# A new written-out order for a transformer block: another order table, a table of buffer slots, 75 operations on other engines, and another split of w_mod's rows over the partitions

## The chip, the cores and the metric

The kernel runs on one core of a Trainium2 chip. The metric is the device time of one execution in microseconds (us). A core has five instruction queues: TensorE (PE, with its weight loads, PEld), ScalarE (ACT), VectorE (DVE), GpSimd (POOL) and SyncE (SP), which here only issues DMA transfers; ACT issues a few DMAs too. Each queue runs in the order in which it was written, and an instruction whose inputs are not there holds up everything behind it on its queue.

## The reference, cut to what matters

The inputs are bf16: x is 2048 rows by 640, attention has 32 heads of 20 with a causal window of 256 rows, the MLP has 1536 hidden columns.

```python
mod = (silu(c) @ w_mod).reshape(1, 6, 1, 640)      # w_mod: 640 x 3840, c: 1 x 640
sa, ca, ga, sb, cb, gb = mod[:, 0], ..., mod[:, 5]
h = layernorm(x) * (1 + ca) + sa
q, k, v = split_heads(h @ wqkv)                    # 640 -> 3 x 32 x 20
p = softmax(where(0 <= i - j < 256, q @ k.T * 20 ** -0.5, -1e9))
x = x + ga * (merge_heads(p @ v) @ wo)
h = layernorm(x) * (1 + cb) + sb
x = x + gb * ((sigmoid(h @ w_gate) * (h @ w_up)) @ w_down)
```

## The kernel before, in words

The 2048 rows are worked in eight chunks of 256 rows, a = 0 to 7. Each chunk goes through the same stages, and the stages of neighbouring chunks are interleaved so that TensorE always has something to do:

- **Head of the program.** c and the first pieces of w_mod are loaded. A small matmul (L634) puts c onto the partitions as five columns, silu(c) is formed (L636 to L640), and its product with w_mod gives the six modulation rows. Row k of w_mod meets element k of c, so both have to lie on the same partition. The rows of the two gates, ga and gb, go through DRAM and come back broadcast to all partitions: `gate<-gq`, then `gbc<-gate`. ga is multiplied into wo (`wos`, L1253), gb into the twelve 128-row pieces of w_down (`wds`, L1192, 128 x 640 each); w_down is needed only by the last matmul of a chunk.
- **LN and modulation.** Statistics on DVE (L776, L778), the power on POOL (L781 to L788), the normalised rows (L793, L796), a transposing DMA on SP's queue (`hT<-x`, L803) and the scale and shift of each transposed piece (`amodu` for attention, `bmodu` for the MLP: L811 on ACT, L812 on DVE).
- **QKV.** `projq`, `projk` and `projv` multiply `hT` by wqkv. The results leave PSUM by copies (`evqk`, `evv`: L893 on ACT, L894 on DVE) into `stg`, `QT`, `KT` or `V`; from `stg`, queries and keys are transposed by DMA on SP's queue.
- **Scores.** For each half of the heads (q = 0, 1) a chunk forms four sets of scores, a block of 24 or 32 small matmuls each (`S<-QT,KT`, L669). There is one PSUM buffer `S` for scores: a set can be written only when the exponentials (L1015, ACT) of the set before it have read it. POOL masks the exponentials (L1040). P times V is one burst of 64 matmuls (`M<-E,V`), joined in one instruction group with the first score set of the next half.
- **Normalising and the way to wo.** DVE transposes, divides and transposes back (L1082, L1087, L1089, L1091). The heads are then regrouped through DRAM: four DMAs a half write `doc<-On` (`n_ow`), two DMAs a chunk read `oT<-doc` on SP's queue, the first (128-row tiles 0 and 1) after the first half, the second (tiles 2 to 4) after both. For chunk 0 the eight writes are issued from ACT's queue. Then comes `wo` (`M<-wo,oT`, five matmuls for 128 rows and 320 columns) and the residual (L1164).
- **MLP.** `mlpg` and `mlpu` (`M<-h2T,wg`, `M<-h2T,wu`) fill two of four PSUM banks M; ACT takes the tanh that stands for the sigmoid (L1209), DVE the product (`glu`, L1211, `hh<-sig,M`), which frees them; `down` (`M<-wd,hh`) and the second residual (L1230) end the chunk.

Projections, matmuls of wo and the MLP stand between the score sets to cover the exponentials.

What sets the order: the program is recorded as 2121 operations (907 for PE, 333 for ACT, 424 for DVE, 264 for POOL, 193 for SP). The table `PRIO` holds one number for each; sorted, they give one order of the whole program, and the remainder by 5 names the engine. `schedule()` goes through the operations in that order and appends each to its engine's queue. It also keeps estimated times (durations, the constants `SWITCH`, `OVERLAP`, `QMAX`, `MIXED`, `START`), which serve one purpose only: where a tile has several buffers it takes the one that these estimates free first. `emit()` then writes the queues and puts semaphore waits on what is not ordered already.

Of the kernel before, what the change touches and what calls it, by code (L numbers as in the profile page):

```python
# [17 lines left out]
NDT = D // 128  # L18
# [7 lines left out]
SWITCH = 0.095  # L26
ENGATTR = {"pe": "tensor", "act": "scalar", "dve": "vector", "pool": "gpsimd", "sp": "sync"}
ENGS = ("pe", "act", "dve", "pool", "sp")
OVERLAP = {"pe": 0.0, "act": 0.085, "dve": 0.075, "pool": 0.045, "sp": 0.0}
# [52 lines left out]
class Prog:  # L82
# [69 lines left out]
    def schedule(self):  # L152


        free = {e: START for e in ENGS}
        bw = 0.0
        lastturn = False
        order = {e: [] for e in ENGS}
        dmacnt = [0] * NDMA
        dmalast = [None] * NDMA  # L160
        rr = 0
        pemode = 0
        portend = 0.0
        freed = {}

        def slot_time(pool, s):
            ten = pool.tenant[s]
            if ten is None:
                if not all(x.done for x in pool.init[s]):
                    return None  # L170
                return max([x.end + x.lat for x in pool.init[s]], default=0.0)
            return None if ten.left else freed[ten]

        def take(t, s):
            ten = t.pool.tenant[s]
            t.prev = list(t.pool.init[s]) if ten is None else list(ten.rel)
            t.slot = s
            t.pool.tenant[s] = t

        for o in sorted(self.ops, key=lambda x: x.prio):  # L180
            assert all(d.done for d in o.deps), o.tag
            e = ENGS[o.prio % 5]
            assert e in o.engs, (o.tag, e)
            o.eng = e
            st = max([o.tmin, free[e] + (SWITCH if e == "pe" and o.mode != pemode else 0.0)]
                     + [d.end + (0.0 if d.eng == "pe" and e == "pe" else d.lat) for d in o.deps])
            if o.isdma and e == "sp":
                st = max(st, bw - QMAX)
            for t in o.tiles:
                if t.slot is None:  # L190
                    step = 1 if t.mate is None else 2
                    best = None
                    for s in range(0, len(t.pool.tenant), step):
                        rts = [slot_time(t.pool, s + k) for k in range(step)]
                        if None not in rts and (best is None or max(rts) < best[0]):
                            best = (max(rts), s)
                    assert best is not None, (o.tag, t.name)
                    if t.mate is None:
                        take(t, best[1])
                    else:  # L200
                        take(t, best[1] + t.odd)
                        take(t.mate, best[1] + 1 - t.odd)
                for x in t.prev:
                    st = max(st, x.end + x.lat)
            if e == "dve" and o.port:
                st = max(st, free["pool"])
            elif e == "pool":
                st = max(st, portend)
            o.start = st
            if e == "pe":  # L210
                pemode = o.mout
            dur = o.dur[e]
            free[e] = st + dur - OVERLAP[e]
            if e == "dve" and o.port:
                portend = free[e]
            if o.isdma:
                turn = o.dlat > 3.0
                if e == "sp" and bw - st > 2.0:
                    free[e] += 0.35 if o.dur[e] > 1.0 else 0.1
                bw = max(st + o.dlat, bw + (MIXED if turn != lastturn and bw > st + o.dlat else 0.0)) + o.work  # L220
                lastturn = turn
                o.end = max(bw - 0.83, st + dur)
                s = rr
                rr = (rr + 1) % NDMA
                dmacnt[s] += 16
                o.key, o.val = f"d{s}", dmacnt[s]
                if dmalast[s] is not None:
                    o.deps.append(dmalast[s])
                dmalast[s] = o
            else:  # L230
                o.end = st + dur
            order[e].append(o)
            o.done = True
            for t in o.tiles:
                t.left -= 1
                if t.left == 0:
                    last = {}
                    for x in t.ops:
                        if x.isdma:
                            last[x] = x  # L240
                    for e2 in ENGS:
                        xs = [x for x in t.ops if x.eng == e2 and not x.isdma]
                        if xs:
                            last[e2] = max(xs, key=lambda x: x.start)
                    t.rel = list(last.values())
                    freed[t] = max(x.end + x.lat for x in t.rel)
        self.order = order
        self.span = max(o.end for o in self.ops)
# [88 lines left out]
def c_pe(n):  # L337
# [3 lines left out]
PE_EPS = 0.14  # L341
PRIO = [
# [124 lines left out]
START = 0.8  # L467
PORTLAG = 0.05
MIXED = 0.55
# [837 lines left out]
```

## Time and profile before

| what | value |
|---|---|
| median of 3 runs | 325.76 us (325.64 to 326.33) |
| span of the profiled execution | 324.3 us, granted clock 1.000 |
| what lies around the span | 325.76 - 324.3 = about 1.5 us |
| PE busy | 317.3 us, 98% |
| ACT, DVE, POOL busy | 212.3 (65%), 211.8 (65%), 187.2 us (58%) |
| DMA | 71694 packets, 37.85 MB |

The span counts from the first to the last instruction of the profiled execution; the measured time also holds what lies around it. Busy shares are averages over stages that differ: the first 90 us load weights and fill the pipeline, the middle is steady, and the last is a tail without new attention work. In a row of the timeline the first number is the start in us, the second the length, and the bracket gives the idle time just before it with the instruction that ended it. Lines are those of the kernel before.

### The profile page before, as it was taken

How to read it: one execution, taken by the hardware profiler on the slowest of the kernel's cores; microseconds unless marked ns; L12 is line 12 of the kernel's file. 1: busy time of each engine (PE TensorE's matmuls, PEld its weight loads, DVE VectorE, ACT ScalarE, POOL GpSimd, SP SyncE). 2: the span in 40 equal slices, each digit the busy share in tenths (PEclk: the TensorE clock that was granted, in tenths of full speed). 3: DMA queues.
4: the chain of work that ended last, by engine and by line, in shares of the span. 5: the costliest groups of instructions: out<-in, count | busy, mean ns of one | idle time of the engine just before them, and what ended most of it. 6: DMA issues, size and time to landing. Idle time of an engine off the chain costs nothing.

```text
span 324.3 us, 11594 instructions
## 1 busy us (share of the span) xinstructions
PE 317.3 (98%) x4872; PEld 222.7 (69%) x4873; DVE 211.8 (65%) x424; ACT 212.3 (65%) x316; POOL 187.2 (58%) x276
## 2 busy tenths in 40 slices
PE   8999999989999999999999999999999999999997
PEld 3564545446776568765776467877786788787885
DVE  5797898778687959674477475837463769264332
ACT  1899985889876687788687867786767764011120
POOL 5128869976668694847585939382939691012100
DMA  7998799989891383824405394340213032202101
GB/s 249 371 333 299 165 269 180 200 137 183 260 164 22 83 109 77 152 61 101 85 22 82 97 103 110 92 69 5 81 40 88 3 79 53 76 20 64 40 2 40
DMA packets 71694, 37.85 MB, mean 117 GB/s; under 512 B 45274, under 2 KB 70362, under 8 KB 71642
## 3 DMA queue, kind: packets, MB, share of 16 engines
q1 hardware_dynamic: 69616, 35.31, 48.3%
q10 hardware_dynamic: 2026, 1.80, 2.1%
q8 instruction: 38, 0.62, 0.8%
q14 instruction: 14, 0.11, 0.1%
HBM read 21.30 MB, written 5.25 MB: 82 GB/s over the span
## 4 chain that ended last, share of the span: by engine, by line
PE 73%; DMA 2%; SPq 2%; DVE 1%; POOL 1%; issue 0%; DVEq 0%
PE M L668 61%; PE S L669 6%; PE M L669 5%; DMA gbc<-gate 2%; SPq L803 2%; DVE wd L1192 1%; POOL x L793 0%; POOL st L788 0%; DVE hh L1211 0%; POOL E L1040 0%; DVE x L1230 0%; DVEq L310 0%
## 5 line engine op out<-in xcount | busy, mean ns | idle before, releaser
L1040 POOL TENSOR_SCALAR_AFFINE_SELECT E<-E 128x512 bf16<-128x512 bf16 (+1 forms) x176 | 142.6, 836 | 68.7 <-ACT E L1015 67.0
L1015 ACT ACTIVATE E<-S 128x512 bf16<-128x512 f32 (+2 forms) x184 | 150.9, 878 | 47.4 <-PE S L669 46.5
L668 PE MATMUL M<-wqkv,hT 128*128 128x480 bf16 (+1 forms) x340 | 73.9, 355 | 0.6 <-ACT hT L846 0.5
L668 PE MATMUL M<-h2T,wu 128*128 128x256 bf16 x480 | 68.0, 273 | 0.5 <-DVE hh L1211 0.5
L668 PE MATMUL M<-h2T,wg 128*128 128x256 bf16 x480 | 67.8, 273 | 0.0
L668 PE MATMUL M<-wd,hh 128*128 128x320 bf16 (+2 forms) x396 | 58.1, 295 | 0.0
L1209 ACT ACTIVATE sig<-M 128x512 f32<-128x512 f32 x48 | 28.9, 602 | 44.1 <-PE M L668 41.7
L1211 DVE SCALAR_TENSOR_TENSOR hh<-sig,M 128x512 bf16<-128x512 f32 x48 | 32.4, 681 | 37.1 <-ACT sig L1209 24.0
L668 PEld LDWEIGHTS M<-h2T,wu 128*128 128x128 bf16 x480 | 45.9, 98 | 8.4 <-issue 1.2
L668 PEld LDWEIGHTS M<-h2T,wg 128*128 128x128 bf16 x480 | 45.7, 98 | 7.1
L668 PEld LDWEIGHTS M<-wqkv,hT 128*128 128x128 bf16 x340 | 30.1, 98 | 27.6 <-DMA wqkv<-in_A_wqkv_dram 1.6
L668 PEld LDWEIGHTS M<-wd,hh 128*128 128x128 bf16 x396 | 36.8, 98 | 14.3 <-DVE hh L1211 0.2
L669 PEld LDWEIGHTS S<-QT,KT 20*64 20x64 bf16 (+1 forms) x1856 | 19.9, 100 | 21.3 <-ACT E L1015 12.0
L1230 DVE TENSOR_TENSOR x<-M,x 128x320 bf16<-128x320 f32 (+2 forms) x33 | 15.6, 476 | 27.2 <-PE M L668 27.2
L669 PE MATMUL S<-QT,KT 20*64 20x256 bf16 (+5 forms) x1856 | 32.1, 228 | 1.2 <-ACT E L1015 1.2
L776 DVE BATCH_NORM_STATS2 st<-x 128x6 f32<-128x320 bf16 x64 | 28.6, 477 | 2.3 <-DMA x<-in_A_x_dram 1.9
L1082 DVE STREAM_TRANSPOSE T<-M 128x512 f32<-128x512 f32 x32 | 21.5, 698 | 9.2 <-PE S L669 8.0
L668 PE MATMUL M<-wo,oT 128*128 128x320 bf16 x160 | 25.4, 299 | 0.0
L669 PE MATMUL M<-E,V 128*32 128x128 bf16 (+1 forms) x960 | 22.8, 246 | 0.8 <-ACT E L1015 0.4
L781 POOL TENSOR_SCALAR st<-st 128x2 f32<-128x2 f32 x16 | 3.7, 234 | 33.8 <-DVE st L778 33.6
L669 PEld LDWEIGHTS M<-E,V 128*32 128x32 bf16 x960 | 19.2, 97 | 5.3 <-issue 2.9
L1091 DVE STREAM_TRANSPOSE On<-Tn 128x1024 bf16<-128x1024 bf16 x16 | 19.8, 1240 | 0.3
(77 smaller groups left out, 240.2 us busy)
## 6 DMA issues: line engine op xcount, KB each, us to landing
x<-in_A_x_dram SPq DMA_DIRECT2D x23, 160.0 KB, 2.3
doc<-On SPq DMA_DIRECT2D x56, 40.0 KB
wd<-in_B_w_down_dram SPq DMA_DIRECT2D x4, 480.0 KB
wd<-in_w_mod_dram SPq DMA_DIRECT2D x5, 320.0 KB
wqkv<-in_A_wqkv_dram SPq DMA_DIRECT2D x4, 400.0 KB
wu<-in_w_mod_dram SPq DMA_DIRECT2D x5, 320.0 KB
oT<-doc SPq DMA_DIRECT2D x8, 192.0 KB, 2.5
out_dram<-x SPq DMA_DIRECT2D x9, 160.0 KB
```

Source lines behind the costliest of these rows:

```text
L668: return e.matmul(o, l, r, start=st, stop=sp, skip_group_check=True)
L669: return e.matmul(o, l, r, start=st, stop=sp, tile_position=tp, skip_group_check=True)
L776: A("dve", lambda e, g, bi=bi, j=j: e.bn_stats(v(bi * 12 + j * 6, 6), src[bi].ap[:, j * 320:(j + 1) * 320]), 0.48, reads=[src[bi].r()], wr ...
L781: A("pool", lambda e, g: e.tensor_scalar(v(28, n), var(), EPS, None, op0=ALU.add), 0.2, reads=[st.r(("m", bi)) for bi in range(n)], writes ...
L803: return e.dma_start_transpose(dst(), src())
L1015: A("act", lambda e, eng: e.activation(dst(), src(), ACT.Exp, scale=SM_SCALE), c_act(n), reads=[Sp.r()], writes=[E.r(key)], prio=3, tag=f" ...
L1040: A("pool", lambda e, eng: e.affine_select(rows(dst), rows(src), pattern=[[0, 8], [sign, n]], compare_op=ALU.is_ge, fill=0.0, base=base, c ...
L1082: A("dve", lambda e, g, h=h: e.transpose(T1.ap[:, 512 * h:512 * h + 512], X[h].ap), 0.694, reads=[X[h].r()], writes=[T1.r(h)], prio=3.5, t ...
L1091: A("dve", lambda e, g: e.transpose(On.ap[:], Tn.ap[:]), 1.22, reads=[Tn.r()], writes=[On.r()], prio=4, tag=f"tr2_{a}")
L1209: A("act", lambda e, g, pg=pg, sg=sg: e.activation(sg.ap[:], pg.ap[:], ACT.Tanh, scale=0.5), c_act(512), reads=[pg.r()], writes=[sg.r()], ...
L1211: A("dve", lambda e, g, pu=pu, sg=sg, f0=f0: e.scalar_tensor_tensor(out=hh.ap[:, f0:f0 + 2, :], in0=sg.ap[:].rearrange("p (a b) -> p a b", ...
L1230: A("dve", lambda e, g, ps=ps, bi=bi, c0=c0, n=n: e.tensor_tensor(x1[bi].ap[:, c0:c0 + n], ps.ap[:, 0:n], x1[bi].ap[:, c0:c0 + n], op=ALU. ...
```

## The change

Three things change.

**Order and engines.** `PRIO` is another table. 75 operations are on another engine, all of them among `evqk`, `evv`, `evqt`, `amodu`, `bmodu`, `ahTe` and one `wds`. PE keeps 907 operations and SP 193; ACT goes from 333 to 331, DVE from 424 to 433, POOL from 264 to 257. SP's queue is word for word the same. On every engine the first 21 us of the program keep their order.

**Slots.** A second table `SLOTS` names the buffer of each tile; the estimates in `schedule()` and their constants are gone.

**c and w_mod.** c is read as 128 pieces of five elements in place of five pieces of 128; w_mod's row 5p+t lies on partition p in column block t, where before row 128t+p lay there. Sizes and numbers of w_mod's pieces stay, their distance in DRAM becomes 5 rows of 7680 bytes instead of one.

```diff
 def schedule(self):
-    free = {e: START for e in ENGS}
...
     for o in sorted(self.ops, key=lambda x: x.prio):
         e = ENGS[o.prio % 5]
-        st = max([o.tmin, free[e] + (SWITCH if e == "pe" and o.mode != pemode else 0.0)]
-                 + [d.end + (0.0 if d.eng == "pe" and e == "pe" else d.lat) for d in o.deps])
...
         for t in o.tiles:
             if t.slot is None:
-                step = 1 if t.mate is None else 2
-                best = None
...
+                s = SLOTS[tiles[t]] if SLOTS else 0
+                ten = t.pool.tenant[s]
+                t.prev = list(t.pool.init[s]) if ten is None else list(ten.rel)
+                t.slot = s
+                t.pool.tenant[s] = t
...
 PRIO = [
-    23, 28, 258, 8, 43, 33, 718, 18, 1218, 38, 3, 507, 513, 72, 67, 48, 53, 58, 76, 84, 101, 99, 144, 149, 154, 159,
+    23, 28, 258, 8, 43, 33, 958, 18, 1448, 38, 3, 507, 513, 72, 67, 48, 53, 58, 76, 84, 101, 99, 144, 149, 154, 159,
...
+SLOTS = [
...
-    c_row = p_oT.aps[0][0:NDT, 0, 0:128]
+    c_pt = p_oT.aps[0][:, 0, 0:NDT]
...
-    dma(lambda: c_row, lambda: c.rearrange("o (t p) -> (o t) p", p=128), 0.05, writes=[R_crow], prio=-1, eng="act", lat=0.3)
-    wm_src = w_mod.rearrange("(t p) f -> p t f", p=128)
+    dma(lambda: c_pt, lambda: c.rearrange("o (p t) -> (o p) t", t=NDT), 0.05, writes=[R_cpt], prio=-1, eng="act", lat=0.3)
+    wm_src = w_mod.rearrange("(p t) f -> p t f", t=NDT)
...
-    e.matmul(psc.ap[:, 0:NDT], c_row, ident[0:NDT, 0:NDT], start=True, stop=True)
+    e.matmul(psc.ap[:, 0:NDT], ident[:], c_pt, start=True, stop=True)
```

Three places of the new order follow. The first is TensorE, the second half of chunk 1's scores (from about 42.6 us in the profile of before): an edge set of 32 score matmuls, two sets of 24, and the projections (`M<-wqkv,hT`) between them. Before:

```order
L669 MATMUL S<-QT,KT 128x64 x32
L668 MATMUL M<-wqkv,hT 128x480 x15
L669 MATMUL S<-QT,KT 64x256 x8
L669 MATMUL S<-QT,KT 64x192 x8
L669 MATMUL S<-QT,KT 64x64 x8
L668 MATMUL M<-wqkv,hT 128x480 x9
L669 MATMUL S<-QT,KT 64x256 x8
L669 MATMUL S<-QT,KT 64x192 x8
L669 MATMUL S<-QT,KT 64x64 x8
L668 MATMUL M<-wqkv,hT 128x480 x15
```

And now:

```order
L635 MATMUL S<-QT,KT 128x64 x32
L634 MATMUL M<-wqkv,hT 128x480 x12
L635 MATMUL S<-QT,KT 64x256 x8
L635 MATMUL S<-QT,KT 64x192 x8
L635 MATMUL S<-QT,KT 64x64 x8
L634 MATMUL M<-wqkv,hT 128x480 x12
L635 MATMUL S<-QT,KT 64x256 x8
L635 MATMUL S<-QT,KT 64x192 x8
L635 MATMUL S<-QT,KT 64x64 x8
L634 MATMUL M<-wqkv,hT 128x480 x13
```

The projections between the sets are 12, 12 and 13 matmuls in place of 15, 9 and 15.

The second place is ScalarE at the same time, about 45 to 53 us: the exponentials (`E<-S`), copies out of PSUM, and the four writes `doc<-On` of chunk 0's second half. Before:

```order
L893 ACTIVATE stg<-M 128x16x20
L893 ACTIVATE V<-M 128x8x20
L1015 ACTIVATE E<-S 128x4x2x192
L1015 ACTIVATE E<-S 128x8x64
L570 DMA doc<-On 20x4x256 x4
L1015 ACTIVATE E<-S 128x8x64
L1015 ACTIVATE E<-S 128x4x2x192
L893 ACTIVATE stg<-M 128x24x20
```

And now:

```order
L981 ACTIVATE E<-S 128x8x64
L981 ACTIVATE E<-S 128x4x2x192
L859 ACTIVATE V<-M 128x24x20
L981 ACTIVATE E<-S 128x8x64
L981 ACTIVATE E<-S 128x4x2x192
L536 DMA doc<-On 20x4x256 x2
L859 ACTIVATE V<-M 128x24x20
L536 DMA doc<-On 20x4x256
L981 ACTIVATE E<-S 128x8x64
L536 DMA doc<-On 20x4x256
L981 ACTIVATE E<-S 128x4x2x192
```

Before, all four writes stand behind the exponentials of the first set of 24 after the edge set. Now two stand behind those of the second, one behind a copy, and the last behind the first half of the exponentials of the third set.

The third place is VectorE from about 80 us: the products of chunk 0's MLP (`hh<-sig,M`), the scaling of w_down (`wd<-wd,gbc`), and the transposes (`T<-M`) that begin the normalising of chunk 2's first half. Before:

```order
L1211 SCALAR_TENSOR_TENSOR hh<-sig,M 128x512
L1192 TENSOR_TENSOR wd<-wd,gbc 128x640 x4
L1211 SCALAR_TENSOR_TENSOR hh<-sig,M 128x512 x3
L1192 TENSOR_TENSOR wd<-wd,gbc 128x640 x4
L1082 STREAM_TRANSPOSE T<-M 128x512 x2
L1211 SCALAR_TENSOR_TENSOR hh<-sig,M 128x512
```

And now:

```order
L1177 SCALAR_TENSOR_TENSOR hh<-sig,M 128x512
L860 CAST stg<-M 128x16x20
L860 CAST V<-M 128x8x20
L1158 TENSOR_TENSOR wd<-wd,gbc 128x640
L1177 SCALAR_TENSOR_TENSOR hh<-sig,M 128x512
L1158 TENSOR_TENSOR wd<-wd,gbc 128x640
L742 BN_STATS st<-x 128x6
L1177 SCALAR_TENSOR_TENSOR hh<-sig,M 128x512
L1158 TENSOR_TENSOR wd<-wd,gbc 128x640 x2
L1177 SCALAR_TENSOR_TENSOR hh<-sig,M 128x512
L1158 TENSOR_TENSOR wd<-wd,gbc 128x640
L742 BN_STATS st<-x 128x6
```

One scaling of w_down stands ahead of the second product where four stood; behind these rows come four more scalings and then the two transposes, so that nine stand ahead of the transposes in place of eight, with two statistics among them.

More of the change, by code (lines that the diff above doesn't have):

```diff
@@ L25 @@
 NDMA = 24
-SWITCH = 0.095
 ENGATTR = {"pe": "tensor", "act": "scalar", "dve": "vector", "pool": "gpsimd", "sp": "sync"}
 ENGS = ("pe", "act", "dve", "pool", "sp")
-OVERLAP = {"pe": 0.0, "act": 0.085, "dve": 0.075, "pool": 0.045, "sp": 0.0}
 class Res:
@@ L152, in schedule @@
     def schedule(self):
-        free = {e: START for e in ENGS}
-        bw = 0.0
-        lastturn = False
         order = {e: [] for e in ENGS}
@@ L161, in schedule, with number @@
         rr = 0
[L162 to L178, printed above, removed]
+        tiles = {}
+        def number(t):
+            if t is not None and t not in tiles:
+                tiles[t] = len(tiles)
+                number(t.mate)
+        for o in self.ops:
+            for t in o.tiles:
+                number(t)
         for o in sorted(self.ops, key=lambda x: x.prio):
@@ L184, in schedule @@
             o.eng = e
-            st = max([o.tmin, free[e] + (SWITCH if e == "pe" and o.mode != pemode else 0.0)]
-                     + [d.end + (0.0 if d.eng == "pe" and e == "pe" else d.lat) for d in o.deps])
-            if o.isdma and e == "sp":
-                st = max(st, bw - QMAX)
             for t in o.tiles:
                 if t.slot is None:
-                    step = 1 if t.mate is None else 2
-                    best = None
[L193 to L215, printed above, removed]
-            if o.isdma:
[L217 to L223, printed above, removed]
-                rr = (rr + 1) % NDMA
[L225 to L231, printed above, removed]
+                    s = SLOTS[tiles[t]] if SLOTS else 0
@@ new lines, in schedule @@
+                    ten = t.pool.tenant[s]
+                    assert ten is not None or all(x.done for x in t.pool.init[s]), (o.tag, t.name)
+                    assert ten is None or ten.left == 0, (o.tag, t.name)
+                    t.prev = list(t.pool.init[s]) if ten is None else list(ten.rel)
+                    t.slot = s
+                    t.pool.tenant[s] = t
+            if o.isdma:
+                dmacnt[rr] += 16
+                o.key, o.val = f"d{rr}", dmacnt[rr]
+                if dmalast[rr] is not None:
+                    o.deps.append(dmalast[rr])
+                dmalast[rr] = o
+                rr = (rr + 1) % NDMA
@@ L237, in schedule @@
                     last = {}
[L238 to L244, printed above, removed]
+                    for x in sorted(t.ops, key=lambda x: x.prio):
+                        last[x if x.isdma else x.eng] = x
                     t.rel = list(last.values())
-                    freed[t] = max(x.end + x.lat for x in t.rel)
         self.order = order
-        self.span = max(o.end for o in self.ops)
     def emit(self):
@@ L338, in c_pe @@
     return max(n, 64) / 2400.0 + 0.0027
-PE_EPS = 0.14
 PRIO = [
[3 rows of a table removed]
[3 rows of a table added]
     92, 87, 187, 237, 242, 247, 253, 263, 272, 267, 280, 275, 290, 300, 305, 286, 317, 296, 322, 311, 376, 357, 386,
[1 row of a table removed]
[1 row of a table added]
     541, 495, 501, 665, 677, 480, 485, 491, 565, 570, 576, 545, 551, 630, 652, 525, 555, 561, 625, 660, 681, 685,
[111 rows of a table removed]
[111 rows of a table added]
+]
+SLOTS = [
[20 rows of a table added]
 ]
@@ L466 @@
 DSAFE = 1.5
-START = 0.8
-PORTLAG = 0.05
-MIXED = 0.55
 NPB = 0
@@ L484 @@
 WSE = (("dve", "pool"), ("dve", "pool"))
-QMAX = 4.5
 WDT = 72.0
@@ L558, in build @@
     R_w3 = [R(f"wqkv{i}") for i in range(12)]
-    R_crow, R_ident, R_ccol, R_cth, R_siluc, R_silubc, R_wo = (R(n) for n in ("crow", "ident", "ccol", "cth", "siluc", "silubc", "wo"))
+    R_cpt, R_ident, R_ccol, R_cth, R_siluc, R_silubc, R_wo = (R(n) for n in ("cpt", "ident", "ccol", "cth", "siluc", "silubc", "wo"))
     R_wg = [[R(f"wg{t}_{h}") for t in range(NDT)] for h in range(2)]
@@ L633, in build @@
     psc = Tile(p_M, "psc")
-    p_oT.init[0].append(A("pe", lambda e, g: e.matmul(psc.ap[:, 0:NDT], c_row, ident[0:NDT, 0:NDT], start=True, stop=True), 0.1,
-      reads=[R_crow, R_ident], writes=[psc.r()], prio=0, lat=0.2, tag="ctr"))
+    p_oT.init[0].append(A("pe", lambda e, g: e.matmul(psc.ap[:, 0:NDT], ident[:], c_pt, start=True, stop=True), 0.1,
+      reads=[R_cpt, R_ident], writes=[psc.r()], prio=0, lat=0.2, tag="ctr"))
     A("dve", lambda e, g: e.tensor_scalar(c_col[:], psc.ap[:, 0:NDT], 0.5, None, op0=ALU.mult), 0.17, reads=[psc.r()], writes=[R_ccol], prio=0)
```

250 rows, old and new, of tables (PRIO, SLOTS) are left out of this document.

## The prediction

> **What bounds the kernel now.** I read the page first: who is busy, and for how long.
>
> ```profile
> span 324.3 us, 11594 instructions
> PE 317.3 (98%) x4872; PEld 222.7 (69%) x4873; DVE 211.8 (65%) x424; ACT 212.3 (65%) x316; POOL 187.2 (58%) x276
> ```
>
> TensorE works 317.3 of 324.3 us. The matmuls are the same after the change, so an order can win only from the 7.0 us in which PE is idle. Where these lie is told by the table of windows (second to fourth number: length, PE busy, PE loads; then DVE, ACT, POOL, clock, DMA share, GB/s):
>
> ```profile
> 0.00:10.00 10.00, 8.35 (x76) 4.11 (x77) 5.56 (x19) 2.62 (x6) 4.73 (x25) 1.00 0.81 269
> 40.00:56.00 16.00, 15.83 (x245) 7.96 (x248) 14.55 (x34) 12.05 (x18) 12.93 (x19) 1.00 1.05 223
> 56.00:72.00 16.00, 14.43 (x275) 7.78 (x271) 12.35 (x24) 12.78 (x19) 14.17 (x20) 1.00 1.00 167
> 72.00:90.00 18.00, 17.49 (x288) 12.71 (x292) 13.70 (x27) 15.84 (x25) 11.29 (x15) 1.00 0.97 225
> 90.00:322.00 232.00, 231.90 (x3640) 172.59 (x3628) 140.07 (x264) 141.78 (x201) 127.92 (x174) 1.00 0.35 69
> 322.00:324.40 2.40, 0.00 (x0) 0.00 (x0) 0.24 (x1) 0.00 (x0) 0.00 (x0) 1.00 0.33 99
> ```
>
> From 90 to 322 us PE is idle for 0.1 us: nothing can be won there, and whatever is won or lost before 90 us comes out at the end unchanged. The head (1.65 us idle) and the tail (2.4 us) keep their order. What is left are the waits between 20 and 92 us. All rows of PE's timeline there that show idle time before them:
>
> ```profile
> 38.23 0.84 PE L669 MATMUL M<-E,V 128*32 128x256 bf16 x32 [0.35 <-DVE hT L858]
> ...
> 48.66 0.43 PE L669 MATMUL S<-QT,KT 20*64 20x256 bf16 x24 [0.17 <-ACT E L1015]
> ...
> 61.60 0.43 PE L669 MATMUL S<-QT,KT 20*64 20x256 bf16 x24 [0.27 <-ACT E L1015]
> ...
> 64.13 0.43 PE L669 MATMUL S<-QT,KT 20*64 20x256 bf16 x24 [0.30 <-ACT E L1015]
> ...
> 67.91 0.43 PE L669 MATMUL S<-QT,KT 20*64 20x256 bf16 x24 [0.42 <-ACT E L1015]
> ...
> 70.48 1.50 PE L669 MATMUL M<-E,V 128*32 128x128 bf16 x64 [0.42 <-ACT E L1015]
> ...
> 86.54 1.25 PE L668 MATMUL M<-h2T,wu 128*128 128x256 bf16 x10 [0.51 <-DVE hh L1211]
> ```
>
> Together 2.44 us: that is about all that this change can win. Six of the seven stand at scores or P times V, five of them for exponentials on ACT; the last is for a product on DVE. Less than 0.2% (0.65 us) could not be told from no change by a measurement of this kernel.
>
> **The change part by part.** The sum is made against the profiled execution (span 324.3 us); 1.5 us lie around it in the median of 325.76.
>
> *c and w_mod.* c is loaded long before it is used, in these rows of the start:
>
> ```profile
> 0.79 0.57 ACTq L570 DMA_DIRECT2D oT<-in_c_dram  x1
> 1.31 2.74 PE L649 MATMUL S<-E 128*128 128x512 bf16 x6 [1.31 <-DVE E L644]
> 3.98 0.18 PE L634 MATMUL M<-ident,oT 5*128 5x5 bf16 x1
> 8.11 0.47 PE L668 MATMUL S<-silubc,wd 128*128 128x64 bf16 x10 [0.19 <-DMA wd<-in_w_mod_dram]
> ```
>
> It is issued at 0.79, and the matmul that takes it runs at 3.98 with no wait, straight behind warm-up matmuls. 128 pieces of 10 bytes in place of five of 256 have some 2.6 us behind their issue. If that cover were too short, the head would move by what is missing. w_mod moves the same bytes in the same pieces; PE waits 0.19 us for it at 8.11, so a slower read shows at once. No row has w_mod read at the new distance. I take 0, with -0.2 (that wait gone) and +0.3 (about twice that wait) as ends. [...]
>
> *75 operations on another engine.* DVE gets nine more, ACT two fewer, POOL seven fewer. One such copy on DVE is
>
> ```profile
> L894 DVE CAST stg<-M 128x480 bf16<-128x480 f32 (+1 forms) x25 | 14.8, 602 | 7.9 <-PE M L668 7.8
> ```
>
> so nine cost at most 9 x 0.6 = 5.4 us of DVE, and the window from 90 to 322 us alone has 232 - 140 = 92 us of DVE idle. Where they fall before 90 us they are in the walk below. By themselves: 0.
>
> *Chunk 1's scores, 40 to 56 us.* Before the set at 48.66 only nine projections stand:
>
> ```profile
> 46.49 2.00 PE L668 MATMUL M<-wqkv,hT 128*128 128x480 bf16 x9
> ```
>
> They take 2.00 us, and PE then waits 0.17 us for the exponentials. Twelve take 2.00 x 12/9 = 2.7 us, more than the wait: it goes. The twelve ahead of the set before (15 until now) still take 2.7 us, and the edge exponentials that they have to cover take 2.06 (row below): no new wait. -0.17, with 0 as the other end.
>
> *The second half of chunk 1 and the first of chunk 2, 56 to 72 us.* Four waits, 1.41 us. The sets, their exponentials and their one buffer are the same, and ACT sets the pace:
>
> ```profile
> 59.49 2.06 ACT L1015 ACTIVATE E<-S 128x512 bf16<-128x512 f32 x4 [0.72 <-PE S L669]
> ...
> 63.97 2.07 ACT L811 ACTIVATE hT<-hT,mA 128x256 bf16<-128x256 bf16 x4
> 65.93 1.92 ACT L1015 ACTIVATE E<-S 128x1536 bf16<-128x1536 f32 x2
> ```
>
> The four modulations at 63.97 stay on ACT between two sets' exponentials, split two and two. Their 2.07 us are still on ACT's chain, so the waits stay, though not at the same rows. I take 0; the ends are -0.7 (half of the waits) and +0.3 (one more such wait).
>
> *Chunk 0's regrouped heads, 46 to 57 us.* The writes move back on ACT's queue. Rows of ACT, SP and PE now, and the page's row of the DMA:
>
> ```profile
> 46.73 1.35 ACTq L570 DMA_DIRECT2D doc<-On  x3
> 48.12 0.40 ACTq L570 DMA_DIRECT2D doc<-On  x1
> ...
> 49.73 3.38 SPq L570 DMA_DIRECT2D oT<-doc  x2
> 53.16 0.48 SPq L570 DMA_DIRECT2D wg<-in_B_w_gate_dram  x1
> ...
> 57.06 1.52 PE L668 MATMUL M<-wo,oT 128*128 128x320 bf16 x10
> ...
> oT<-doc SPq DMA_DIRECT2D x8, 192.0 KB, 2.5
> ```
>
> The last write is issued at 48.12. SP's second read of `oT` is issued just before 53.1, some 4.6 us later, since it waits until the write has landed; 2.5 us after that it is there, at about 55.2, and wo begins at 57.06. In the new order the last write stands behind half of the third set's exponentials. That set starts at about 51.6 (48.5, + 0.4 for the set before, + 13 x 2.00/9 = 2.9 for the projections, less some 0.2 of overlap), its exponentials follow 0.5 us behind: I estimate the issue at 52.1, four us later than now. wo now stands behind five projections, not two, so PE reaches it at about 57.06 + 3 x 0.2 - 0.17 = 57.5. The read has to be issued by 57.5 - 2.5 = 55.0, that is, the write may take 2.9 us. With 4.6 us it would be late by 1.7 us. What the 4.6 consists of isn't seen in a row; DMA is fully busy then (share 1.05 in the window 40 to 56). The view of SP's waits (us in total, times, longest) has three of that kind in the whole trace:
>
> ```profile
> SPq L310 <- DMA doc<-On: 5.0, 3, 2.4
> ```
>
> I take 0 (a write under 2.9 us: no wait for one is over 2.4), with +1.7 as the end. [...]
>
> *Chunk 0's MLP, 72 to 97 us.* The chain of waits runs through the gate's row:
>
> ```profile
> 77.92 5.14 DMA gbc<-gate
> ...
> 83.16 1.28 DVE wd L1192 x2
> ...
> 85.72 0.69 DVE hh L1211
> ```
>
> Four scalings of w_down stand ahead of the product that PE waits for. DVE's timeline there:
>
> ```profile
> 83.16 2.65 DVE L1192 TENSOR_TENSOR wd<-wd,gbc 128x640 bf16<-128x640 bf16 x4 [2.12 <-DMA gbc<-gate]
> 85.72 1.27 DVE L1211 SCALAR_TENSOR_TENSOR hh<-sig,M 128x512 bf16<-128x512 f32 x2
> 87.89 0.69 DVE L1211 SCALAR_TENSOR_TENSOR hh<-sig,M 128x512 bf16<-128x512 f32 x1 [0.89 <-PE M L668]
> 88.49 1.69 DVE L1192 TENSOR_TENSOR wd<-wd,gbc 128x640 bf16<-128x640 bf16 x4
> 91.01 1.31 DVE L1082 STREAM_TRANSPOSE T<-M 128x512 f32<-128x512 f32 x2 [0.82 <-PE S L669]
> ...
> 93.07 0.44 DVE L776 BATCH_NORM_STATS2 st<-x 128x6 f32<-128x320 bf16 x1
> ```
>
> With one scaling ahead of it the product comes some 1.8 us earlier and the 0.51 us are gone. What is late next is DVE itself. Ahead of the transposes that stand at 91.01 now come nine scalings, not eight, and two statistics. From 83.16 to 90.18 DVE was busy for 7.02 - 0.89 = 6.1 us; with 0.4 for a scaling (1.69/4) and 2 x 0.44 it is 7.4, so the transposes come at about 83.16 + 7.4 = 90.6, against 91.01. They free the banks of PSUM that the MLP takes next. So of the 0.5 us about 0.4 to 0.5 get through: -0.5. Ends: 0, if DVE keeps all of it, and -1.0, if `gbc` lands earlier with the rest and the wait at its next place shrinks too.
>
> *After 90 us.* The sets are spread more evenly among the matmuls, but PE was idle 0.1 us: 0, up to +0.4 if one set stands badly (as the 0.42 at 67.91).
>
> *Sum:* 0 + 0 - 0.17 + 0 + 0 - 0.5 + 0 = -0.67 us, span 323.6 us, and 325.76 - 0.67 = 325.1 us as a median. Its own ends, without the late read and the larger gain: 324.5 (the last two gains at half of their way to the lower end) and 325.8 (both lost).
>
> **The rivals.**
>
> *The read of `oT` for chunk 0 is late (slower).* It decides once the last write takes over 2.9 us to land. With 4.6 as now, PE stands 1.7 us at wo, and the four transposing loads behind the read on SP's queue move back too, those for chunk 4's `hT` among them, which ACT's modulations need. -0.67 + 1.7 = +1.0: 326.8 us, and with another 0.3 for these, 327.1. For it: the same write took 4.6 us in a window with all DMA busy. Against: one instance.
>
> *The gate's row is the bound (no change).* If `gbc` lands at 83.1 as now, or later by 0.3, DVE's ten or eleven scalings push the transposes to 91 and the 0.5 us is not had: 325.6 to 325.8 us.
>
> *More of the waits goes.* Half of the 1.41 us between 56 and 72, the 0.17, and the whole of the late term: -0.7 - 0.17 - 1.0 = -1.9, 323.9 us. For it: the sets' distances are evened throughout. Against: ACT's chain there has the same work.
>
> **How the numbers follow.** Forecast 0.42: of its range 324.5 to 325.8 somewhat more than half lies below 325.11 (faster by over 0.2%), 0.24, and 0.18 within. More waits gone 0.16, all faster. Gate's row 0.09, within. Late read 0.33, slower by over 0.2% nearly always. Faster 0.40, same 0.27, slower 0.33. The likeliest is 325.1 us. The range reaches from 323.8 (the larger gain) to 327.0 (the late read at 4.6 us); what lies outside is the late read with its loads, and small tails.
>
> **What would show it.** PE's timeline: no wait at the second set of 24 in chunk 1's second half (48.5), four waits that sum to about 1.4 us between 56 and 72, none at the `wu` row near 86, DVE's transposes near 90.5. SP: second `oT<-doc` issued by 55 and wo at 57.5 without a wait. The forecast is wrong if PE shows idle time at `M<-wo,oT` for DMA `oT<-doc`; if the waits of 56 to 72 shrink by half; if idle appears after 90 us; or if the first 20 us are not the same within 0.3 us.

## The result, and the profile after

The changed kernel is slower: 330.4 us, the median of six executions (329.33 to 331.86 in five of them), against 325.76 (325.64 to 326.33), a ratio of 1.0136 with a 95% interval of 1.0112 to 1.0160. A second measurement (e1 below) gave 331.25 us, ratio 1.0188 (1.0161 to 1.0215). The sixth execution lasted 1104 us, with TensorE busy for 1098 us in place of 319 (its first six matmuls took 5.06 us in place of 2.74) while the recorded clock was 1.00; this didn't come back in any run that followed, its cause stays open, and the profile shown here is that of e1, the same kernel in an ordinary execution of 330.83 us. Line numbers are lower by 34 than before; the experiments' own are shifted a little further.

The page: span, and who is busy.

```profile
span 329.0 us, 11572 instructions
...
PE 319.2 (97%) x4872; PEld 222.6 (68%) x4873; DVE 216.9 (66%) x433; ACT 213.4 (65%) x314; POOL 182.6 (55%) x269
```

The span is 4.7 us longer than 324.3. PE's idle time is 329.0 - 319.2 = 9.8 us in place of 7.0, and PE is busy for 319.2 in place of 317.3 although it does the same matmuls. Both have to be explained. The windows, with the same columns as before:

```profile
40.00:56.00 16.00, 16.00 (x254) 8.08 (x252) 13.48 (x32) 12.59 (x19) 13.40 (x20) 1.00 0.96 199
56.00:72.00 16.00, 12.76 (x193) 6.08 (x182) 9.79 (x23) 13.04 (x19) 14.15 (x21) 0.96 0.99 177
72.00:90.00 18.00, 18.00 (x296) 12.45 (x294) 12.84 (x24) 13.20 (x20) 9.86 (x11) 0.94 0.94 218
90.00:322.00 232.00, 230.99 (x3649) 170.67 (x3647) 147.62 (x271) 145.24 (x205) 123.41 (x167) 1.00 0.36 70
```

From 56 to 72 us PE now stands idle for 3.24 us (1.57 before), and the granted clock, 1.00 everywhere before, is 0.96 and 0.94 there. From 90 us on it is idle for 1.0 us, where before it was 0.1. PE's timeline from 20 us on, the rows with idle time before them:

```profile
22.83 3.66 PE L634 MATMUL M<-wqkv,hT 128*128 128x480 bf16 x17 [0.28 <-DVE hT L824]
38.30 0.84 PE L635 MATMUL M<-E,V 128*32 128x256 bf16 x32 [0.25 <-DVE hT L824]
58.65 0.41 PE L635 MATMUL S<-QT,KT 20*128 20x64 bf16 x32 [0.31 <-ACT E L981]
64.80 2.81 PE L634 MATMUL M<-wqkv,hT 128*128 128x480 bf16 x12 [0.53 <-DVE st L744]
71.02 2.18 PE L634 MATMUL M<-wqkv,hT 128*128 128x480 bf16 x5 [2.33 <-DVE stg L860]
95.78 0.39 PE L634 MATMUL M<-h2T,wu 128*128 128x256 bf16 x2 [0.59 <-DVE T L1048]
152.94 2.76 PE L634 MATMUL M<-wqkv,hT 128*128 128x480 bf16 x12 [0.29 <-DVE x L1196]
```

The waits for exponentials at 48.66, 61.60, 64.13, 67.91 and 70.48 have gone but for 0.31 us, and so has the one at 86.54. In their place stands one of 2.33 us at 71.02, for a copy `stg<-M` on DVE. DVE's timeline says why that copy is late:

```profile
65.20 0.32 DVE L860 CAST V<-M 128x160 bf16<-128x160 f32 x1
69.56 0.49 DVE L742 BATCH_NORM_STATS2 st<-x 128x6 f32<-128x320 bf16 x1 [4.04 <-DMA x<-in_A_x_dram]
69.97 0.43 DVE L762 TENSOR_SCALAR x<-x,st 128x640 bf16<-128x640 bf16 x1
70.31 1.21 DVE L860 CAST stg<-M 128x480 bf16<-128x480 f32 x2
```

A statistics instruction waits 4.04 us for rows of x to land, and everything behind it on DVE's queue waits with it, the copies among them. These rows are those of chunk 6; PE is at chunk 4's projections. In the old order that instruction stands behind all of chunk 4's projections. SP's queue shows when its load goes out:

```profile
49.84 4.75 SPq L536 DMA_DIRECT2D oT<-doc  x2
54.64 0.48 SPq L536 DMA_DIRECT2D wg<-in_B_w_gate_dram  x1
...
63.04 0.58 SPq L536 DMA_DIRECT2D wu<-in_B_w_up_dram  x1
63.74 0.43 SPq L536 DMA_DIRECT2D x<-in_A_x_dram  x1
```

And in the profile of before:

```profile
61.87 0.44 SPq L570 DMA_DIRECT2D x<-in_A_x_dram  x1
```

The load goes out at 63.74, 1.9 us later, since the second read of `oT`, and all behind it, is later by about 1.5 us. It lands at 69.5, behind 576 KB of w_up. Finer windows behind PE's wait show what it costs besides:

```profile
68.00:70.00 2.00, 0.70 (x3) 0.12 (x3) 0.44 (x2) 1.91 (x2) 1.73 (x4) 1.00 0.52 101
70.00:72.00 2.00, 0.98 (x3) 0.44 (x4) 2.00 (x6) 0.03 (x1) 1.60 (x2) 0.68 0.42 89
72.00:74.00 2.00, 2.00 (x28) 0.91 (x29) 1.02 (x2) 0.57 (x1) 0.00 (x0) 0.50 0.63 125
74.00:76.00 2.00, 2.00 (x75) 1.37 (x68) 0.42 (x1) 0.43 (x1) 0.00 (x0) 0.96 0.68 162
```

The granted clock falls to 0.50 and comes back at about 74. In between PE counts as busy, at half rate: five projection matmuls take 2.18 us in the row at 71.02, where nine took 2.00 before, and P times V behind them takes 1.97 us, where it took 1.50 (70.48). At half rate for some 3 us PE loses about 1.5 us.

### The profile page after: what moved, and what is told of

It reads as the page before. It is cut to its first block, busy times and chain, and to the rows that moved or that the text cites. A ratio compares the mean times of both kernels' runs of the same rounds, so it can differ in the third digit from the quotient of the medians.

```text
span 1102.3 us, 11573 instructions
## 1 busy us (share of the span) xinstructions
PE 1098.3 (100%) x4873; PEld 501.4 (45%) x4873; DVE 216.6 (20%) x433; ACT 218.7 (20%) x314; POOL 179.1 (16%) x269
## 4 chain that ended last, share of the span: by engine, by line
PE 100%; DVE 0%; issue 0%
PE M L634 85%; PE M L635 7%; PE S L635 6%; PE S L615 1%; PE S L634 1%; PE S L626 0%; DVE E L610 0%; DVE x L1196 0%; PE M L600 0%
## 5 line engine op out<-in xcount | busy, mean ns | idle before, releaser
L634 PE MATMUL M<-wqkv,hT 128*128 128x480 bf16 (+1 forms) x340 | 253.7, 990 | 0.0
L634 PE MATMUL M<-h2T,wg 128*128 128x256 bf16 x480 | 222.2, 693 | 0.0
L634 PE MATMUL M<-h2T,wu 128*128 128x256 bf16 x480 | 221.5, 679 | 0.0
L634 PE MATMUL M<-wd,hh 128*128 128x320 bf16 (+2 forms) x396 | 205.6, 774 | 0.0
L634 PEld LDWEIGHTS M<-h2T,wg 128*128 128x128 bf16 x480 | 103.5, 217 | 92.0 <-issue 90.0
L634 PEld LDWEIGHTS M<-h2T,wu 128*128 128x128 bf16 x480 | 98.5, 209 | 91.4 <-issue 89.2
L634 PEld LDWEIGHTS M<-wd,hh 128*128 128x128 bf16 x396 | 83.8, 214 | 106.4 <-issue 103.6
L634 PE MATMUL M<-wo,oT 128*128 128x320 bf16 x160 | 87.0, 781 | 0.0
L635 PE MATMUL M<-E,V 128*32 128x128 bf16 (+1 forms) x960 | 75.0, 557 | 0.0
L635 PE MATMUL S<-QT,KT 20*64 20x256 bf16 (+5 forms) x1856 | 69.0, 423 | 0.0
```

The lines of the kernel that those rows point to most:

```text
L634: return e.matmul(o, l, r, start=st, stop=sp, skip_group_check=True)
L635: return e.matmul(o, l, r, start=st, stop=sp, tile_position=tp, skip_group_check=True)
```

## The experiments

**e1 to e3: which edit.** e1 is the changed kernel again. e2 is the kernel before with the edits to c and w_mod alone, e3 the changed kernel with these undone:

```diff
-    wm_src = w_mod.rearrange("(t p) f -> p t f", p=128)
+    wm_src = w_mod.rearrange("(p t) f -> p t f", t=NDT)
...
```

> The changed kernel as it is, for a profile of an execution whose TensorE runs at full rate. All theories: 329 to 331 us. Theory A (the late read of oT, the rival of the prediction): PE idles about 1.7 us or more at the rows M<-wo,oT near 57 us, and most of the 4.6 us stands between 50 and 75 us. Theory B (the head): the first 20 us are longer by some us, with matmuls of the head slower or w_mod's pieces later, and the rest is as before. Theory C (order elsewhere): new idle rows of PE, 0.3 to 1 us each, spread over 40 to 322 us.

> The kernel before with the edits to c and w_mod alone (5p+t), old order and slots. Theory A and C: 325.8 us, no change (within 0.3). Theory B: 329 to 331 us, all of the loss.

> The changed kernel with the edits to c and w_mod undone (128t+p), new order and slots. Theory A and C: 329 to 331 us, all of the loss stays. Theory B: 325.1 us, what the prediction gave for the order.

Measured: e1 331.25 us; e2 325.52, ratio 0.9997 (0.9988 to 1.0007); e3 330.88, ratio 1.0157 (1.0125 to 1.0189). The edits to c and w_mod cost nothing that can be measured; theory B falls. Theory A falls too, by e1's profile: wo starts at 57.50, as forecast, with no wait. The loss stays with e3, that is with order, engines and slots, which e1 to e3 don't separate. In e2's profile one row deserves notice, which the forecast rests on:

```profile
85.81 1.25 PE L668 MATMUL M<-h2T,wu 128*128 128x256 bf16 x10
```

This is the row that in the first profile of the old order stood behind the wait of 0.51 us. Here, in the same order, there is no wait: the gate's row had landed in time.

**e4 to e7: the wait for the load.** Each moves a few instructions of the program in the order, by a list of moves read ahead of the queues (numbers are those of the operations as recorded: 886 the statistics, 881 their load, 381 a normalising step which the new order has just behind two of the copies, 377 a statistics step which the old order has ahead of them, 506 a transposing load on SP in front of w_up's; 354 and 355 to 358 the last transpose of chunk 0's second half and its writes, 267 and 559 a copy on DVE and an exponential on ACT):

```diff
+        for m, after in MOVES:
+            seq.remove(num[m]); seq.insert(seq.index(num[after]) + 1, num[m])
...
+MOVES = ((886, 381),)                                             # e4, in the changed kernel
+MOVES = ((886, 377),)                                             # e5, in the kernel before
+MOVES = ((881, 506),)                                             # e6, in the changed kernel
+MOVES = ((354, 267), (358, 559), (357, 358), (356, 357), (355, 356))  # e7, in the changed kernel
```

> The changed kernel; one statistics instruction on DVE (of the rows of x for chunk 6, whose load lands at about 69.5 us) stands four places later, behind the copies stg<-M and the second normalising of x for chunk 0. Theory S (that instruction waits for its load and holds up DVE's queue, PE's wait of 2.3 us follows, and PE's clock falls after the wait): the 2.3 us and the clock loss of 1 to 2 us go, the 0.5 us at 64.8 stays, 325.4 us (325.0 to 326.0). Theory Q (SP's queue is late because of the moved writes, the statistics only show it): the wait moves to the next instruction that needs something late, 328 us or more.

> The kernel before; only that one statistics instruction is moved ahead on DVE, to about 65.9 us. Theory S: x is issued at 61.9 there, so it lands at about 67.7 and DVE stands 1.8 us; PE then waits some 1 us more: 326.5 us (326.2 to 328). Theory Q: no change, 325.8 us.

> The changed kernel; the statistics stay where they are, but the load of x that they wait for goes one place ahead on SP's queue, in front of a load of w_up of 576 KB. Theory S: it lands some 2 to 3 us earlier, DVE waits about 1 us in place of 4, PE under 0.3 us there, clock 1.0: 325.6 us (325.2 to 326.5). Theory Q: 329 to 331 us, since SP stays as late as it is.

> The changed kernel; the last transpose of chunk 0's second half (DVE) and its four writes (ACT) go back to about the place that they have in the kernel before. SP's second read of oT then goes out some 1.5 to 2 us earlier. Theory S: x lands at about 68, DVE still waits 2.5 us, PE about 0.8, no fall of the clock: 326.5 us (326 to 328). Theory Q: all of it goes, 325.3 us.

Measured: e4 328.03 us (327.38 to 328.17), ratio 1.0062 (1.0047 to 1.0077); e6 328.47, 1.0086 (1.0067 to 1.0105); e7 328.89 (327.57 to 329.48), 1.0098 (1.0080 to 1.0116); e5 325.94, 1.0030 (0.9998 to 1.0062). All four profiles have the clock at 1.00. PE's timeline of e4, the rows with idle time from 69 us on:

```profile
69.78 1.19 PE L642 MATMUL M<-wqkv,hT 128*128 128x480 bf16 x5 [0.45 <-DVE stg L868]
93.07 0.39 PE L642 MATMUL M<-h2T,wu 128*128 128x256 bf16 x2 [0.59 <-DVE T L1056]
150.24 2.76 PE L642 MATMUL M<-wqkv,hT 128*128 128x480 bf16 x12 [0.29 <-DVE x L1204]
```

The 2.33 us are 0.45, and 331.25 - 328.03 = 3.2 us have gone: 1.9 of wait, and the rest with the clock. In e7 SP is on time: x goes out at 61.90 (61.87 before, 63.74 in e1). In e5 it goes out at 62.95, in e6 at 63.98 but ahead of w_up. DVE's waits for the load in e5 and e7, and its statistics in e6, which no longer wait:

```profile
67.40 0.49 DVE L784 BATCH_NORM_STATS2 st<-x 128x6 f32<-128x320 bf16 x1 [0.87 <-DMA x<-in_A_x_dram]
```

```profile
65.85 0.49 DVE L750 BATCH_NORM_STATS2 st<-x 128x6 f32<-128x320 bf16 x1 [0.75 <-DMA x<-in_A_x_dram]
```

```profile
66.43 0.49 DVE L750 BATCH_NORM_STATS2 st<-x 128x6 f32<-128x320 bf16 x1
```

Theory S is right about the cause: moving the instruction back, or its load ahead, or having SP on time, each takes the long wait out of the profile, with order, engines and slots otherwise as they were. It was wrong about what is left, since none came near 325.4; about 2.2 us of the loss are elsewhere. e5 shows something else: its ten executions are six of 325.5 to 326.0, three of 329.1 to 329.4 and one of 327.5. The profile is of the first kind. The granted clock is 1.000 in the three slow ones too, so a fall of the clock isn't what they lose by; a later landing of the load would be a guess, since no profile of one was taken. Theory Q (the lateness of SP alone) fails on e4, which leaves SP as late as it was. For the long wait both are needed: in e7 the statistics stand early and SP is on time, and its profiled wait is 0.75 us; of its other three executions, 328.44 to 329.48 us, there is no profile.

**h1: one of the other waits, mended alone.** The wait of 0.59 us is for the transposes, which on DVE come behind four scalings of w_down. One of these is slow there; DVE's and POOL's timelines of e1:

```profile
92.22 1.27 DVE L1158 TENSOR_TENSOR wd<-wd,gbc 128x640 bf16<-128x640 bf16 x3
93.52 1.57 DVE L1158 TENSOR_TENSOR wd<-wd,gbc 128x640 bf16<-128x640 bf16 x1
95.02 1.30 DVE L1048 STREAM_TRANSPOSE T<-M 128x512 f32<-128x512 f32 x2
```

```profile
93.17 1.57 POOL L1158 TENSOR_TENSOR wd<-wd,gbc 128x640 bf16<-128x640 bf16 x1 [1.61 <-DVE wd L1158]
```

The four take 2.87 us in place of 1.69. Three of them take under half a us each; the fourth, 93.52 to 95.09, takes 1.57 us, and POOL's own scaling runs beside it, 93.17 to 94.74. Whether the one slows the other was not tried. POOL's wait of 1.61 us is another matter: its scaling waits by the program's own semaphore for a piece that DVE scales just ahead. In the profile of before, POOL's scaling starts at 89.87, when DVE's last of four (89.70) already runs. h1 is e4 with the transposes ahead of the four:

```diff
-MOVES = ((886, 381),)
+MOVES = ((886, 381), (829, 883), (830, 829))
```

> As e4 (the one statistics instruction back), and on DVE the two transposes that begin chunk 2's normalising go ahead of four scalings of w_down, where the profiles of the changed kernel show PE idle for 0.59 us behind them. If these scalings cause that wait, it goes and 328.0 becomes 327.3 us. If the transposes are late for another reason (P times V itself, or the gate's row), 328.0 us stays.

It got much worse: 332.42 us, ratio 1.0208 (1.0170 to 1.0246). DVE and PE in its profile:

```profile
91.81 1.31 DVE L1056 STREAM_TRANSPOSE T<-M 128x512 f32<-128x512 f32 x2 [1.90 <-PE S L643]
```

```profile
100.64 1.51 PE L642 MATMUL M<-wo,oT 128*128 128x320 bf16 x5 [2.36 <-DVE x L1138]
```

The 0.59 us are gone, but DVE now stands 1.90 us for P times V ahead of the transposes, the scalings come that much later, and the residual that PE waits for comes behind them. Behind PE's wait matmuls take longer up to about 106 us: five of wo 1.51 us, where the five at 95.21 take 0.84; twelve of w_down 3.41, where eight at 109.70 take 1.26; and a score set at 105.28 takes 0.65, where that at 109.34 takes 0.43. By these rows it costs some 2.4 us more. The mean clock of each of the four executions is 0.989 to 0.995. The scalings in front were filling for time in which DVE had nothing else to do.

**k3 and k5: the clock.** e4 with statistics added on DVE ahead of the copy that PE waits for; they read a weight and write where nothing reads:

```diff
+        if o.seq == 604:
+            def slowed(e, g):
+                for i in range(3):   # k5: 5
+                    e.bn_stats(scr[:, 6 * i:6 * i + 6], wqkv[:, 0, 0:320])
+                return fn(e, g)
```

> As e4, with three added statistics instructions on DVE (they read wqkv and write to a place that nothing reads) ahead of the copy stg<-M near 69 us that PE waits for: about 1.25 us more wait, 1.7 us in all, by an instruction and no load. If PE's clock falls only after a longer wait: 328.0 + 1.25 = 329.3 us, granted clock 1.00 in every window. If any wait of over a us lowers it: 330.5 us or more.

> The same with five added instructions: about 2.1 us more, 2.5 us of wait in all, near the 2.3 us that the changed kernel showed. If the fall of the clock follows the length of PE's idle time: 328.0 + 2.1 + 1.5 = 331.6 us and matmuls at half rate for about 3 us behind the wait. If the fall in the changed kernel had another cause: 330.1 us, clock 1.00.

Measured: k3 330.67 us (329.29 to 331.08), k5 330.40 (329.39 to 331.60). PE's waits of k3 and of k5, and k5's windows behind it:

```profile
70.82 1.19 PE L643 MATMUL M<-wqkv,hT 128*128 128x480 bf16 x5 [1.63 <-DVE stg L869]
```

```profile
71.76 1.19 PE L643 MATMUL M<-wqkv,hT 128*128 128x480 bf16 x5 [2.62 <-DVE stg L869]
```

```profile
72.00:74.00 2.00, 2.00 (x37) 1.26 (x39) 2.00 (x5) 0.57 (x1) 0.14 (x1) 0.76 0.07 14
74.00:76.00 2.00, 2.00 (x64) 1.42 (x56) 0.15 (x1) 0.00 (x0) 0.00 (x0) 0.50 0.77 169
```

k5 shows the fall where the wait is for added instructions and no load: the added instructions alone brought it, in two of the four executions of each kernel (mean clock 0.995, where e4 without them has 1.000 in all four). The medians don't separate the two, because the clock falls in some executions and not in others. By the granted clock of each execution:

| kernel, PE's profiled wait | executions at clock 0.999 to 1.000 | at 0.995 or below |
|---|---|---|
| changed (its timing and e1), 2.33 us | 329.33, 329.51, 329.75 | 330.83, 330.87, 331.05, 331.64, 331.86, 332.65 |
| k3, 1.63 us | 329.29, 330.43 | 330.91, 331.08 |
| k5, 2.62 us | 329.39, 329.86 | 330.95, 331.60 |
| e4, 0.45 us | 327.38 to 328.17 (four) | none |

In the changed kernel the first group's mean is 329.5 us and the second's 331.5, and six executions of nine are in the second. Half rate for some 3 us accounts for 1.5 of these 2 us; whether the rest is a longer wait wasn't seen. The expectation of k3, that a wait of 1.7 us leaves the clock alone, holds for two of its four.

**h2 to h4: where the other 2.2 us are.** Programs joined from the two orders. h2 takes the new order, with the moves of e4 and e7, up to chunk 2's first P times V (about 89 us) and the old behind; h3 the same up to chunk 1's first (about 55 us); h4 the old order up to 89 us and the new behind, with e4's move.

```diff
+p[s] = 5 * i + (new[s] % 5 if s in front else old[s] % 5)   # h2, h3; h4 the other way round
```

> The new order and engines up to chunk 2's first P times V (about 89 us; with the statistics instruction later, and chunk 0's writes early as in e7), then what is left in the old order and on the old engines; slots likewise, and where neither table fits, the buffer free for longest. Theory T (what e4 still loses is lost after 90 us, by single waits of DVE and PE that the new order has there): 325.2 us (324.8 to 325.8). Theory U (the new front leaves less work for later covers, so the loss is there however the rest is ordered): 327 us or more.

> The new order and engines only up to chunk 1's first P times V (about 55 us), with chunk 0's writes early as in e7; everything behind in the old order, on the old engines. If the gain of the new order lies in the waits before 56 us and the losses all lie behind, this beats both: 325.1 us (324.7 to 325.5). If the new front only shifts its waits behind the cut: 325.8 us or more.

> The reverse of h2: the old order and engines up to chunk 2's first P times V (about 89 us), what is left in the new order and on the new engines, the one statistics instruction at its later place. If the new order loses about 2.1 us after 90 us by itself, as the profiles of e4 and e7 have it: 327.9 us (327.3 to 328.4). If that loss was handed on from the new front: 325.8 to 326.3 us.

Measured: h2 326.89 us, ratio 1.0030 (1.0010 to 1.0050); h3 327.07, 1.0042 (1.0027 to 1.0057); h4 327.06, 1.0037 (1.0025 to 1.0050). PE's waits of h4 from 90 us on, and h3's largest:

```profile
92.39 0.39 PE L640 MATMUL M<-h2T,wu 128*128 128x256 bf16 x2 [0.25 <-DVE T L1054]
149.56 2.76 PE L640 MATMUL M<-wqkv,hT 128*128 128x480 bf16 x12 [0.29 <-DVE x L1202]
```

```profile
72.05 1.50 PE L641 MATMUL M<-E,V 128*32 128x128 bf16 x64 [1.72 <-POOL x L765]
```

h4 says that the new order, with its engines and slots, loses 1.2 us behind 89 us by itself, less than the 2.1 expected; the same waits stand in it as in e4, the first of them smaller. h2 is 1.1 us above the kernel before with the old order behind 89 us. It would be wrong to add the two up to e4's 2.2. Chunk 2's first P times V and PE's last row, before and then in e4, say where e4 loses:

```profile
89.03 1.50 PE L669 MATMUL M<-E,V 128*32 128x128 bf16 x64
315.20 6.71 PE L668 MATMUL M<-wd,hh 128*128 128x320 bf16 x60
```

```profile
88.99 1.50 PE L643 MATMUL M<-E,V 128*32 128x128 bf16 x64
316.92 6.71 PE L642 MATMUL M<-wd,hh 128*128 128x320 bf16 x60
```

At 89 us e4 is level with the kernel before. From there to PE's end it takes 234.65 us in place of 232.88, some 1.75 us more, and 0.3 us more lie behind PE's end. So nearly all that e4 still loses lies behind 89 us. The same stretch takes 234.6 to 234.7 us in e1, e3, e7, k3 and k5, and 232.8 to 232.9 in e2, e5, h2 and h3, which have the old order there. PE's idle time makes 1.0 us of the 1.75; the rest are longer steps between matmuls in rows that count as busy, and whether order, engines or slots bring them was not separated. Theory T has the place right and the cause in part. h2's loss is its own:

```profile
43.29 1.34 DVE L1225 TENSOR_TENSOR wo<-wo,gbc 128x640 bf16<-128x640 bf16 x2 [0.51 <-DMA gbc<-gate]
47.99 2.21 PE L640 MATMUL M<-wqkv,hT 128*128 128x480 bf16 x9 [0.38 <-DVE V L866]
```

In its profile DVE stands for the gate's row ahead of a scaling of wo, a copy `V` comes late behind it, and PE waits 0.38 us; the profiles of before and of e1 have no such wait. That explains a part of the 1.1 us only. h3 can't tell what it was meant for: at the seam a normalising step on POOL comes too late for its masks, 1.72 us that neither order has. No version beat the kernel before; e2 equals it.

## Why the prediction was wrong, point by point

- **56 to 72 us (0, with ends -0.7 and +0.3).** This is the step that failed. The four waits for exponentials did go for the most part, against the forecast. But I walked this stretch along ACT's chain and took DVE's part of the new order for copies and residuals; I did not ask of each statistics instruction there which rows it reads and when these are loaded. One of them reads rows that SP asks for at about 62 us, and had been moved ahead of copies that PE needs. The result was a wait of 2.33 us where +0.3 was the upper end, and in six of nine executions a fall of the clock, which costs about 1.5 us more. e4 gave 3.2 us back.
- **The regrouped heads and the late read.** The step was right: the last write was issued at 52.13 (52.1 forecast), the second read of `oT` is out by 54.6 (49.84 + 4.75), and wo starts at 57.50 (57.5 forecast) without a wait. From the end of that write's issue (52.13 + 0.33) to there are 2.1 us, where the rival had 4.6. The rival with the most weight on the slow side did not happen. But I priced the read's delay at wo and at `hT` alone. The load of x stands in the same queue, went out 1.9 us later, and that, with a slower landing (5.8 us behind its issue in e1, 3.95 in e7), made the wait above long (e7: 0.75 us with SP on time).
- **72 to 97 us (-0.5).** The wait at 86.54 is gone, but e2 and others show that the old order doesn't have it in every execution: it depended on one landing of the gate's row. So there was little to win. What I named as late next, DVE's transposes behind nine scalings, was right, but mis-sized: I took 0.4 us for a scaling, and of the last four three took under 0.5 and one 1.57 beside POOL's; the two copies on DVE ahead of the first scaling were left out too. The transposes began at 95.02 in e1 and at 92.31 in e4, where 90.6 was forecast, and a wait of 0.59 us came of it.
- **40 to 56 us (-0.17).** Right: the wait at 48.66 is gone and that window has no idle time left. In some profiles it is offset by a new one at 22.83 (0.28 us in e1, 0.49 in e4, none in e3 and e7), where the new order runs into a projection whose `hT` isn't there.
- **After 90 us (0, up to +0.4).** This term failed too: h4 loses 1.2 us there, and by the traces e1 and e4 lose some 1.75 us from 89 us to PE's end. "PE was idle 0.1 us" says that the old order has no wait, not that a new one won't make any.
- **c and w_mod (0), the engines (0).** The first is shown by e2: 0.9997, with the matmul that takes c at 3.84 without a wait (3.98 before). The pieces of 10 bytes changed nothing that can be measured; that the work in front of that matmul hides what they may cost is likely, and was not tried. The engines were not tried alone, and neither were the slots, which the prediction gave no term.

## What to carry to other kernels

An instruction that is moved ahead on an in-order queue brings its own inputs' times with it (in e1 a wait of 4.04 us on DVE): look up the load behind each moved instruction, its place in its DMA queue and what lies ahead of it there, before looking at what the move wins. The wait of 2.33 us on TensorE could not be priced by its length alone, since the half clock behind it cost about 1.5 us more, and only in six of nine executions. And a wait of some tenths that one profile shows needs a second profile before a gain is booked on it.

## What the runs showed of the hardware

The granted clock fell to 0.50 at PE waits of 2.33 us (e1: 0.68, 0.50 and 0.96 in the windows of 2 us from 70 to 76) and 2.62 us (k5: 0.76, 0.50 and 0.89 from 72 to 78), in each for some 3.4 us by these windows. Behind one of 2.36 us (h1) matmuls took up to 1.8 times as long until about 106 us, and the mean clock of that execution is 0.989. With 1.63 us (k3) two of four executions have a mean clock of 0.995, and with 0.45 us (e4) none is below 1.000. The changed kernel has 0.995 in six of nine executions and 0.999 to 1.000 in three; what decides between them no run shows. A read of 160 KB that stands behind one of 576 KB took 5.8 us from issue to its user's start (63.74 to 69.56 in e1), 3.95 us in the same place in e7 (61.90 to 65.85), and 2.45 us or less with the two exchanged (63.98 to 66.43 in e6). One scaling of 128x640 on DVE took 1.57 us beside one on POOL, and the three ahead of it 1.27 us together (e1).
